# Transposing three more tiles by DMA in a fused chunked-attention and gated feed-forward kernel

## Chip, cores, metric

The kernel runs on one core of one Trainium2 chip, in one launch. The metric is device time in microseconds (us), the median of several runs. TensorE is called PE, VectorE DVE, ScalarE ACT, GpSimd POOL and SyncE SP, as in the profile. POOL, SP and ACT also issue the transfers (DMAs).

## What is computed

Attention over chunks of 32 positions, each with 16 positions to its left, 8 to its right and 8 memory positions, and then a feed-forward layer with a ReLU gate, on every position. 4 batches, 8 heads, 768 positions, head dimension 64; the feed-forward layer has width 512 and inner width 1536.

```python
for c in range(S // 32):
    q_c = q[:, :, 32*c:32*c+32]
    k_full = concat([mem_k, k[:, :, max(0, 32*c-16):min(S, 32*c+40)]], axis=2)
    v_full = concat([mem_v, v[:, :, max(0, 32*c-16):min(S, 32*c+40)]], axis=2)
    scores = q_c @ k_full.T / sqrt(D)
    scores = scores - max(scores)
    a = exp(scores); a = a / (sum(a) + 1e-9)
    out[:, :, 32*c:32*c+32] = a @ v_full
x = out.transpose(0, 2, 1, 3).reshape(B * S, H * D)
result = (relu(x @ w_gate) * (x @ w_val)) @ w_out
```

## The kernel before

The 3072 positions are 24 tiles of 128, six to a batch: tiles 0 to 5 are batch 0, 6 to 11 batch 1, 12 to 17 batch 2, 18 to 23 batch 3. For the feed-forward layer the tiles form eight blocks of 2, 2, 2, 4, 4, 4, 4 and 2 tiles; block 3 is tiles 6 to 9, block 4 tiles 10 to 13, block 5 tiles 14 to 17, block 6 tiles 18 to 21, block 7 tiles 22 and 23.

**Attention of a tile.** q and k are loaded by POOL with a cast to bf16 (`load_qk`, L250). Both must be transposed, so that the head dimension lies across the partitions. There are two ways. In the first, PE transposes by a product with the identity (`qk_t`, L271, four products for q and four for k) into PSUM, and ACT or DVE copies the result out (`qk_copy`, L285). In the second, a transposing DMA that SP issues (`qk_transfer`, L277) does it from on-chip memory to on-chip memory: q straight into `qT`, k into a staging tile `k_t` (three buffers), from which ACT or DVE copies it into the layout of `kT`. Tiles from `LATE_QK` on take the second way. The scores are 32 small products (`scores`, L297); the scores of tile a need k of tile a + 1 too, unless a is the last of its batch. Then come the row maximum, subtraction, exponential, sum, reciprocal and normalisation on DVE and ACT (L314 to L352). The result P is transposed in the same two ways: by PE and a copy (`p_t`, `p_copy`), or, from tile `LATE_P` on, by a transposing DMA (`p_transfer`, L360). `values` (L368) multiplies it by v, and `x_copy` puts the result into the block's xT.

**v.** For batches 1 to 3, v lies in one of two large buffers `v_bd`, used in turn. POOL loads it in four DMAs (`load_v_rows`, L182); then eight small DMAs (`mem_rows`, L164) put the memory rows in; then ACT or DVE copies 24 rows of each chunk up from the next one (`upper`, L190, sixteen copies a batch).

**Feed-forward of a block.** For each of 12 slices of the inner width, PE makes four products for the gate and four for the value (`first`, L401); ACT takes the ReLU (`relu`, L410) and DVE multiplies (`gate`, L415). At the end `second` (L427) makes the output products of every tile, in four groups of three, and ACT copies out and stores (`store`, L435). These products share four PSUM buffers.

**Order.** The order on every engine is fixed before the launch by a list scheduler inside the kernel (`schedule`, L682). It steps through a made-up time with a guessed duration of every operation and, on each engine, takes the ready operation of the best priority. PE, DVE, ACT and SP then run their lists strictly in that order, held by semaphores for true dependences only; the guessed times leave no trace but the order. POOL's order is the list `loads`, written out by hand (L639 to L675): the pairs and weights, then q and k of tile 6 to k of tile 8, the output weights, v of batch 1, then q and k up to k of tile 16, then v and memory rows of batch 2, then q and k of tiles 16 to 22, v and memory rows of batch 3, and the last three loads of q and k.

The names that the change touches:

- `LATE_QK`, `LATE_P` (L56): the tiles from which q, k and P are transposed by DMA.
- `pace` (L508): an operation after which a PE transpose of q or k may be placed: one that stands `LEAD` = 31 us of the planner's time ahead of the block's start.
- `pace_t` (L517): the same for a transposing DMA of tile a: not before the scores of tile a - 6 have been placed.
- `ISSUE`, `LAND`, `LAND_P` (L515): the planner's guesses of how long SP is busy with one transposing DMA, and how long after that its data is there. L770 is the guess of how much each one delays the loads.
- L674: which loads of q and k stand behind which batch's v in POOL's list.

Of the kernel before, what the change touches and what calls it, by code (L numbers as in the profile page):

```python
# [19 lines left out]
def kernel(  # L20
# [32 lines left out]
    BAND0 = 48  # L53
    UT = 3

    LATE_QK, LATE_P = 15, 15  # L56

    KEY_RUNS = ((0, CH, 0), (KW, 64, CH), (CH, KW, CTX))
    assert sum(BLOCKS) == NT and NMEM == 8 and D == 64 and H == 8
# [130 lines left out]
    def upper(b, par, i0, i1, eng):  # L190

        x = v_bd[b % NSET].rearrange("p h c d -> p (h c) d")
        d = slice(D * par, D * par + D)
        copy(eng, x[64 * par + CH:64 * par + CTX, i0:i1, d], x[64 * par:64 * par + CTX - CH, i0 + 1:i1 + 1, d])
# [232 lines left out]
    def second(blk, t, c, m0):  # L427
        st = FFN[blk]
        if m0 == 0:
            st["o", t, c] = fps.tile([128, c[1] - c[0]], F32, tag="fps", name="out_ps")  # L430
        for m in range(m0, m0 + MS):
            nc.tensor.matmul(st["o", t, c], lhsT=st["gv"][:, m, 128 * t:128 * t + 128],  # L432
                             rhs=w_out_sb[:, m, c[0]:c[1]], start=(m == 0), stop=(m == NDC - 1))

    def store(blk, t, c, eng):  # L435
        o = opool.tile([128, c[1] - c[0]], F32, name="o_sb")
        copy(eng, o, FFN[blk].pop(("o", t, c)))
        row = 128 * (starts[blk] + t)
        nc.scalar.dma_start(out[row:row + 128, c[0]:c[1]], o)


    starts = [sum(BLOCKS[:i]) for i in range(len(BLOCKS))]
# [8 lines left out]
    def op(key, eng, fn, deps=(), prio=(0,), take=(), give=(), after=()):  # L451
        ops[key] = dict(eng=eng, fn=fn, deps=list(deps), prio=prio, take=list(take), give=list(give),
                        after=list(after))

    def load(key, n, work, fn, deps=(), take=(), after=()):
        loads.append(dict(key=key, n=n, work=work, fn=fn, deps=list(deps), take=list(take), after=list(after)))
# [39 lines left out]
    LEAD, STEP, AHEAD = 31.0, 5.2, 10.0  # L496
    marks, clock, begun = [], 0.0, {}
# [9 lines left out]

    def pace(a):  # L508
        blk = block_of[a]
        at = begun[blk] - LEAD + STEP * (a - starts[blk]) - (AHEAD if a >= LATE_P else 0.0)  # L510
        gone = [key for c, key in marks if c <= at]
        return gone[-1:] if blk >= 2 else []


    ISSUE, LAND, SLACK, LAND_P = 1.4, 4.5, 1.0, 3.0  # L515

    def pace_t(a):  # L517
        return [("s", a - 6)]

    for a in range(NT):  # L520
        b, t = divmod(a, TPB)
# [48 lines left out]
        blk = block_of[a]  # L570
# [11 lines left out]
    for rank, (blk, m) in enumerate(seq):  # L582
# [11 lines left out]
        else:  # L594
            last = None
            for t, c in [(t, c) for t in range(n) for c in pieces(blk, t)]:
                for m0 in range(0, NDC, MS):
                    end = (t, c, m0) == (n - 1, pieces(blk, t)[-1], NDC - MS)
                    op(("o", blk, t, c, m0), {"PE": MS * 0.000422 * (c[1] - c[0])},
                       lambda e, blk=blk, t=t, c=c, m0=m0: second(blk, t, c, m0),  # L600
# [5 lines left out]
                   lambda e, blk=blk, t=t, c=c: store(blk, t, c, engine[e]), [last], (0.5, rank), ["o"],  # L606
# [11 lines left out]
    for b in range(1, B):  # L618
        for n in range(2 * HP):
            hp, par = divmod(n, 2)  # L620
            for m in range(TPB // UT):
# [3 lines left out]
                   lambda e, b=b, par=par, i0=i0, i1=i1: upper(b, par, i0, i1, engine[e]),  # L625
# [13 lines left out]
    late = [(a, i) for a in range(TPB, NT) for i in (1, 0)]  # L639
# [22 lines left out]
    for b in range(1, B):  # L662
        deps = ([("z0", hp, c0) for hp in range(HP) for c0 in range(0, NCH, 8)] if b > 1 else [("z1", hp) for hp in range(HP)]) + ([("v", TPB * (b - NSET + 1) - 1)] if b > NSET else [])
        if b == 1:
            for n in range(2 * HP):
                op(("mr", b, n), {"SP": 0.72}, lambda e, n=n: mem_rows(nc.sync, 1, n),
                   deps + [(("vm", 0), 0.2), (("vm", 1), 0.2)], (0,))
        for par in range(2):
            load_v_op(b, par, deps)
        if b > 1:  # L670
            for n in range(2 * HP):
                load(("mr", b, n), 192, 0.22, lambda b=b, n=n: mem_rows(nc.gpsimd, b, n),
                     deps + [(("vm", 0), 0.2), (("vm", 1), 0.2)])
        for a, i in late[5 if b == 1 else 9 + 12 * (b - 1):21 + 12 * (b - 1)]:  # L674
            load_qk_op(a, i)  # L675

    WARM = 18.0
# [4 lines left out]
    def schedule():  # L682
        done, started, times = {}, set(), [0.7]
        free = {e: 0.7 for e in ("PE", "ACT", "DVE", "SP", "POOL")}
        queue_end, flying, gives = 0.0, [], [(WARM + 0.15, "fps")]
# [28 lines left out]
        while len(started) < len(ops) + len(loads):  # L714
            t = heapq.heappop(times)
            while times and times[0] <= t + 1e-9:
                heapq.heappop(times)
            for g in [g for g in gives if g[0] <= t + 1e-9]:
                gives.remove(g)
                room[g[1]] += 1  # L720
            flying = [f for f in flying if f > t]
            moved = True
            while moved:
                moved = False
                for e in ("POOL", "PE", "ACT", "DVE", "SP"):
                    if free[e] > t + 1e-9:
                        continue
                    if e == "POOL":
                        if n_load == len(loads):
                            continue  # L730
                        o = loads[n_load]
                        if len(flying) >= 8 or not ready(o, t):
                            continue
                        n_load += 1
                        key = o["key"]
                        if o["n"]:
                            end = t + 0.62 + 0.27e-3 * o["n"]
                            queue_end = max(queue_end, end + 0.8) + o["work"]
                            flying.append(queue_end + 1.0)
                            done[key] = queue_end + (1.2 if n_load < 8 else 4.5 if key[:2] == ("vl", 1) else 2.4 if n_load < 45 else 6.0 if key[0] == "vl" else 4.0)  # L740
                        else:
                            end = done[key] = t + max(o["work"], 0.6)
                        fn = o["fn"]
                    else:
                        o = None
                        soon = False
                        for _, key in todo[e]:
                            late_pe = e == "PE" and t > 36.0 and ops[key]["prio"][0] == 1
                            if ready(ops[key], t, MARGIN if late_pe else 0.0):
                                o = None if soon and key[0] in ("up", "z0") else ops[key]  # L750
                                break
                            soon = soon or ready(ops[key], t + 0.3)
                        if o is None:
                            if e == "PE" and 1.3 < t < WARM:
                                order.append((t, lambda: idle_product(256)))
                                free[e] = t + (0.213 if t < 9.0 else 0.11)
                                heapq.heappush(times, free[e])
                            elif e == "PE" and t <= 1.3:
                                heapq.heappush(times, 1.31)
                            continue  # L760
                        for x in o["eng"]:
                            todo[x].remove((o["prio"], key))
                        d = o["eng"][e]
                        d, lat = d if isinstance(d, tuple) else (d, d)
                        d *= (1.8 if e == "PE" and t < 8.0 and key[0] in ("t", "p", "sh", "f") else 1.0)
                        end = t + d
                        done[key] = end + 0.25 if e == "PE" else t + lat + 0.08

                        if queue_end > t:
                            queue_end += 1.1 if e == "SP" and key[0] in ("t", "pc") else 0.7 if key[0] == "oc" else 0.0  # L770
                        fn = lambda o=o, e=e: o["fn"](e)
                        for g in o["give"]:
                            g, lag = g if isinstance(g, tuple) else (g, 0.0)
                            gives.append((done[key] + lag, g))
                            heapq.heappush(times, done[key] + lag)
                    for r in o["take"]:
                        room[r] -= 1
                    started.add(key)
                    for k in users.get(key, ()):
                        missing[k] -= 1  # L780
                        if not missing[k]:
                            offer(k)
                    order.append((t, fn))
                    free[e] = end
                    for x in (end, done[key], done[key] + 0.2, done[key] + 1.5, done[key] + MARGIN):
                        heapq.heappush(times, x)
                    moved = True
            assert times, [k for k in ops if k not in started][:20]
# [34 lines left out]
```

## Time and profile before

| | |
|---|---|
| median of 3 runs | 244.66 us (244.35 to 244.89) |
| the profiled execution | 244.74 us |
| its span, first to last instruction | 242.7 us |
| last product on PE ends | 239.6 us into the span |
| granted clock of PE, mean | 0.998 |
| PE busy | 235.8 us (97%) |
| DVE, ACT busy | 147.9 us, 136.0 us |
| POOL busy (it issues the loads) | 77.9 us |
| transposing DMAs on SP: q and k of tiles 15 to 23, P of the same | 18 and 9 |
| first and last of them issued | 71.98 us, 164.3 us |
| last load of q issued by POOL | 122.45 us |

The profile is one execution. "Idle before" gives what an engine waited for; a timeline lists instructions by start time, with the number merged into a line behind an x. A queue such as SPq or POOL lists the issue of a DMA, not its landing. A block's first products start at about 85.7 (block 3), 122.4 (block 4), 160.0 (block 5), 192.6 (block 6) and 223.7 us (block 7).

### The profile page before, as it was taken

What the parts mean: (1) busy time and instruction counts of PE and PEld (TensorE: products, weight loads), DVE (VectorE), ACT (ScalarE), POOL (GpSimd) and SP (SyncE); (2) the same over time, 40 slices, a digit from 0 to 9 for tenths busy, and PEclk for the clock granted to TensorE, in tenths of its full rate; (3) what the DMA queues carried; (4) which work ended last, traced back from release to release, by engine and by line L of the source; (5) the groups of instructions that cost most, each with busy time, mean ns of one, the idle gap of its engine ahead of it and who ended that gap; (6) DMA issues with size and microseconds to landing.
All of it is one profiled execution on the core that took longest, in us unless ns stands there. A gap on an engine that the chain in (4) does not pass through costs nothing.

```text
span 242.7 us, 6546 instructions
## 1 busy us (share of the span) xinstructions
PE 235.8 (97%) x2706; PEld 140.8 (58%) x2706; DVE 147.9 (61%) x296; ACT 136.0 (56%) x288; POOL 77.9 (32%) x102
## 2 busy tenths in 40 slices
PE   7898999999999999999999999999999999999994
PEld 5587887884589545554544545554445444445873
DVE  6674876988877458977549999894431043410430
ACT  7477777767885499665756674453332233312432
POOL 8975689235984396037430000000000000000000
PEclk9999999999999999999999999999999999999999
DMA  6999999999999999999990142651001210012102
GB/s 72 172 179 203 201 164 172 193 131 134 191 195 154 80 168 136 120 124 153 116 218 7 36 53 48 131 133 24 0 0 46 86 43 0 3 43 86 43 3 86
DMA packets 96413, 25.17 MB, mean 104 GB/s; under 512 B 87424, under 2 KB 93312, under 8 KB 96384
## 3 DMA queue, kind: packets, MB, share of 16 engines
q0 software_dynamic: 76128, 14.65, 83.5%
q1 hardware_dynamic: 16656, 3.82, 15.0%
q10 hardware_dynamic: 3600, 6.29, 8.1%
q8 instruction: 21, 0.34, 0.7%
q14 instruction: 8, 0.07, 0.1%
HBM read 28.55 MB, written 6.29 MB: 144 GB/s over the span
## 4 chain that ended last, share of the span: by engine, by line
PE 88%; ACT 4%; DMA 2%; POOL 2%; DVE 2%; issue 1%; ACTq 0%; POOLq 0%
PE v_ps L407 26%; PE g_ps L407 25%; PE out_ps L432 22%; PE xT_ps L388 3%; DMA v_n<-in_v_dram 2%; PE s_ps L309 2%; PE idle_ps L141 2%; PE vs_ps L215 2%; PE xT_ps L381 2%; PE pT_ps L358 2%; ACT v_bd L79 1%; PE qk_ps L275 1%; PE qk_ps L236 1%; POOL qk_p L227 1%; ACT o_sb L79 1%
## 5 line engine op out<-in xcount | busy, mean ns | idle before, releaser
L419 DVE TENSOR_TENSOR gvT<-v_ps,g_relu 128x256 f16<-128x256 f32 (+1 forms) x96 | 52.9, 554 | 58.2 <-PE v_ps L407 43.2
L407 PE MATMUL v_ps<-xT,w_val_sb 128*128 128x256 f16 (+1 forms) x384 | 78.2, 326 | 0.1
L407 PE MATMUL g_ps<-xT,w_gate_sb 128*128 128x256 f16 (+1 forms) x384 | 78.2, 326 | 0.0
L413 ACT ACTIVATE g_relu<-g_ps 128x256 f16<-128x256 f32 (+1 forms) x96 | 47.0, 491 | 47.6 <-PE g_ps L407 45.9
L432 PE MATMUL out_ps<-w_out_sb,gvT 128*128 128x512 f16 (+2 forms) x300 | 65.3, 371 | 0.0
L407 PEld LDWEIGHTS <-w_gate_sb 128*128 128x128 f16 x384 | 36.3, 98 | 23.1
L407 PEld LDWEIGHTS <-w_val_sb 128*128 128x128 f16 x384 | 36.0, 98 | 22.3 <-issue 0.5
L432 PEld LDWEIGHTS <-gvT 128*128 128x128 f16 x300 | 27.9, 98 | 29.9
L79 ACT COPY o_sb<-out_ps 128x512 f32<-128x512 f32 (+2 forms) x25 | 14.2, 567 | 31.8 <-PE out_ps L432 25.6
L337 ACT ACTIVATE p_exp<-dif 128x256 f16<-128x256 f32 (+2 forms) x72 | 19.6, 340 | 4.4 <-DVE dif L329 3.5
L322 DVE TENSOR_REDUCE mx<-s_ps 128x8 f32<-128x512 f32 x24 | 16.5, 688 | 5.6 <-PE s_ps L309 5.4
L341 DVE TENSOR_REDUCE sm<-p_exp 128x8 f32<-128x512 f16 x24 | 16.4, 683 | 4.4 <-ACT p_exp L337 4.1
L254 POOL DMA_DIRECT2D qk_b<-in_q_dram x18 | 16.4, 912 | 7.4 <-DMA v_bd<-in_v_dram 5.5
L254 POOL DMA_DIRECT2D qk_b<-in_k_dram x18 | 16.2, 903 | 5.5 <-DMA w_out_sb<-in_moe_w_out_dram 4.4
L79 ACT COPY v_bd<-v_bd 24x768 f16<-24x768 f16 (+1 forms) x20 | 15.6, 818 | 2.2 <-ACT o_sb L79 1.2
L352 DVE TENSOR_TENSOR p_n<-p_exp,rinv 128x512 f16<-128x512 f16 x24 | 16.5, 687 | 0.4
L329 DVE TENSOR_TENSOR dif<-s_ps,mx 128x512 f32<-128x512 f32 x24 | 16.4, 682 | 0.2
L185 POOL DMA_DIRECT2D v_bd<-in_v_dram x12 | 10.9, 920 | 12.5 <-PE v_ps L407 11.8
L168 POOL DMA_DIRECT2D v_bd<-vmem x16 | 10.5, 661 | 12.5 <-DMA v_bd<-in_v_dram 10.5
L79 ACT CAST xT<-xT_ps 128x512 f16<-128x512 f32 x17 | 9.9, 583 | 6.2 <-PE xT_ps L388 4.8
L141 PE MATMUL idle_ps<-idle 128*128 128x256 bf16 x69 | 11.5, 319 | 1.1 <-DVE warm L475 1.1
L388 PEld LDWEIGHTS <-v_bd 128*128 128x128 f16 x288 | 9.7, 96 | 3.2 <-issue 0.2
(57 smaller groups left out, 179.5 us busy)
## 6 DMA issues: line engine op xcount, KB each, us to landing
out_dram<-o_sb ACTq DMA_DIRECT2D x23, 256.0 KB
qk_b<-in_k_dram POOLq DMA_DIRECT2D x18, 128.0 KB, 7.2
qk_b<-in_q_dram POOLq DMA_DIRECT2D x18, 128.0 KB, 7.0
v_bd<-in_v_dram POOLq DMA_DIRECT2D x6, 384.0 KB, 11.5
w_out_sb<-in_moe_w_out_dram POOLq DMA_DIRECT2D x2, 768.0 KB, 10.5
qk_p<-in_k_dram POOLq DMA_DIRECT2D x3, 256.0 KB, 5.7
qk_p<-in_q_dram POOLq DMA_DIRECT2D x3, 256.0 KB, 6.6
v_n<-in_v_dram POOLq DMA_DIRECT2D x6, 128.0 KB, 6.5
```

The source lines that it names most:

```text
L79: nc.scalar.copy(o, i)
L254: nc.gpsimd.dma_start(qk_b[a, i], bass.AP(tensor=x.tensor, offset=x[b, 0, 128 * t, 0].offset, ap=[[D, 128], [S * D, H], [1, D]]))
L322: nc.vector.reduce_max(SM[a, "mx"], s4, axis=AX.X)
L329: nc.vector.tensor_tensor(out=SM[a, "dif"].rearrange("p (m r) a s -> p r m a s", r=2), in0=S_ps.pop(a).rearrange("p r (m a) s -> p r m a s ...
L337: nc.scalar.activation(p[:, :, :, s0:s0 + k1 - k0], dif[:, :, :, k0:k1], ACT.Exp, scale=SCALE)
L341: nc.vector.reduce_sum(SM[a, "sm"], SM[a, "p"], axis=AX.X)
L352: nc.vector.tensor_tensor(out=P_n[a], in0=SM.pop((a, "p")), in1=rinv_b, op=ALU.mult)
L388: nc.tensor.matmul(ps[:, hp, r], lhsT=v_bd[b % NSET][:, hp, 4 * t + g, :], rhs=x[:, hp, r], start=True, stop=True)
L407: nc.tensor.matmul(ps, lhsT=w[:, f, 128 * m:128 * m + 128], rhs=xTs[blk][:, f, :], start=(f == 0), stop=(f == NFC - 1))
L413: nc.scalar.activation(st["r", m], st.pop((0, m)), ACT.Relu)
L419: nc.vector.tensor_tensor(out=st["gv"][:, m, :], in0=st.pop((1, m)), in1=st.pop(("r", m)), op=ALU.mult)
L432: nc.tensor.matmul(st["o", t, c], lhsT=st["gv"][:, m, 128 * t:128 * t + 128], rhs=w_out_sb[:, m, c[0]:c[1]], start=(m == 0), stop=(m == ND ...
```

## The change

Tiles 12, 13 and 14, too, have q, k and P transposed by DMA: six more transposing DMAs of q and k and three of P, 36 in place of 27, and 36 products fewer on PE. In POOL's list, v and the memory rows of batch 2 move ahead of the nine loads from k of tile 12 to k of tile 16; all loads from tile 12 on to k of tile 22 now follow them in one run of 21. The PE transposes of tiles 10 and 11 may be placed 44 instead of 31 us of planner's time ahead of block 4, and a transposing DMA of tile a as soon as the scores of tile a - 3 are placed. Three guesses of the planner grow. It alone decides what follows for the order of all else.

```diff
-    LATE_QK, LATE_P = 15, 15
+    LATE_QK, LATE_P = 12, 12
...
     def pace(a):
         blk = block_of[a]
-        at = begun[blk] - LEAD + STEP * (a - starts[blk]) - (AHEAD if a >= LATE_P else 0.0)
+        at = begun[blk] - (44 if blk >= 4 else LEAD) + STEP * (a - starts[blk]) - (AHEAD if a >= LATE_P else 0.0)
         gone = [key for c, key in marks if c <= at]
         return gone[-1:] if blk >= 2 else []
...
-    ISSUE, LAND, SLACK, LAND_P = 1.4, 4.5, 1.0, 3.0
+    ISSUE, LAND, SLACK, LAND_P = 1.5, 6.0, 1.0, 6.0
...
     def pace_t(a):
-        return [("s", a - 6)]
+        return [("s", a - 3)]
...
-        for a, i in late[5 if b == 1 else 9 + 12 * (b - 1):21 + 12 * (b - 1)]:
+        for a, i in late[(5, 12, 33)[b - 1]:(12, 33, 36)[b - 1]]:
             load_qk_op(a, i)
...
                         if queue_end > t:
-                            queue_end += 1.1 if e == "SP" and key[0] in ("t", "pc") else 0.7 if key[0] == "oc" else 0.0
+                            queue_end += 1.5 if e == "SP" and key[0] in ("t", "pc") else 0.7 if key[0] == "oc" else 0.0
```

The order that results on PE, from block 3's last product on (f b,m: gate, value = the two product groups of slice m of block b; s, v, p: scores, values and PE transposes of P; t: PE transposes of q or k; o: output products):

```
before: o 3 (with p13, v13) | f 4,0 gate, t14q, value | f 4,1 | s14 | f 4,2 | f 4,3 gate, s15, value | ...
after:  o 3 (with v13, s16, s17, v14, v15) | f 4,0 gate, s18, value | f 4,1 | f 4,2 gate, v16, value, s19 | f 4,3 gate, v17, value | ...
```

And SP's list of transposing DMAs (k, q, P of a tile):

```
before: k15 q15 k16 q16 k17 q17 k18 q18 k19 q19 k20 q20 k21 q21 k22 q22 P15 k23 q23 P16 P17 ... P23
after:  k12 q12 k13 q13 k14 q14 k15 q15 k16 q16 P12 k17 P13 q17 k18 q18 P14 P15 k19 q19 k20 P16 q20 P17 k21 ...
```

## The prediction

> **What bounds the kernel now.** I read the page first (busy times, slices), then the chain of waits, then the timelines of POOL and SP, and last the DMA view of single stretches, for the transfers that the change adds to.
>
> ```profile
> span 242.7 us, 6546 instructions
> PE 235.8 (97%) x2706; PEld 140.8 (58%) x2706; DVE 147.9 (61%) x296; ACT 136.0 (56%) x288; POOL 77.9 (32%) x102
> DMA  6999999999999999999990142651001210012102
> ```
>
> PE has hardly any idle time; the other engines have much. DMA (40 slices of 6.07 us) is full to about 127 us and nearly empty after. The change takes work from the first and gives it to the second while that is full. The chain of waits from 120 to 135 us is PE alone:
>
> ```profile
> 122.57 0.86 PE g_ps L407 x4
> 123.43 0.22 PE qk_ps L275 x4
> 123.65 0.86 PE v_ps L407 x4
> ...
> 126.24 0.24 PE s_ps L309 x32
> 126.48 0.97 PE g_ps L407 x4
> ...
> 134.19 0.23 PE pT_ps L358 x4
> ```
>
> Four transposing products hold PE for 0.22 or 0.23 us, and nothing waits on either side. So work taken from PE here shortens the end by as much, as long as what PE needs next is there.
>
> **Part 1: 36 products off PE.** Six groups of q and k at 0.22 and three of P at 0.23: **2.0 us**. [...] The copies that go with them (ACT row of pT 586 ns, x3, and of qT) come off ACT and DVE, which are not the bound: nothing.
>
> **Part 2: tiles 10 and 11 sooner.** Their PE transposes and scores move from block 3's time (86.5 us on) into block 2's (about 72 to 81 us). PE is full in both, so the move itself is worth nothing. Their softmax (row maximum, subtraction, sum, normalisation at 0.69 each, the reciprocal at 0.2: 2.9 us of DVE a tile) goes along; DVE is busy 4.5 of the 8 us from 76 to 84, which hides it. Without that cover it would cost up to 5.8 - 3.5 = 2.3 us. I take 0.
>
> **Part 3: v of batch 2 past nine loads of q and k in POOL's queue.**
>
> ```profile
> 58.73 0.91 POOL L254 DMA_DIRECT2D qk_b<-in_k_dram  x1
> ...
> 67.46 3.80 POOL L185 DMA_DIRECT2D v_bd<-in_v_dram  x4 [0.52 <-DVE p_n L352]
> 71.25 0.67 POOL L168 DMA_DIRECT2D v_bd<-vmem  x1
> ...
> 84.26 0.92 POOL L254 DMA_DIRECT2D qk_b<-in_q_dram  x1
> ```
>
> The first line is k of tile 12, the last q of tile 16. The zeroing that v waits for ends on DVE at 55.6, so v can be issued at 58.7, four DMAs in 3.8 us. Then come the memory rows, which wait for v to land, as they do here (four waits, 10.5 us). Loads alone bring 11801 packets in the 12 us from 56 to 68, 983 a us; v is 6144 packets, so 6.3 us after q of tile 11 (landed 64.4 by the completion records), plus a latency of 1.3: about 72. So k of tile 12 is issued near 72.7 (71 to 75) and lands 4.3 later, at 77, as q of tile 16 does here (84.26, landed 88.6). It then stands where q of tile 16 stands now, 11.5 us sooner. Nothing on PE is due from it before 90: 0.
>
> **Part 4: the transposing DMAs, at the time when the loads run.** SP's timeline and the DMA view of the stretches 92 to 100 (loads and transposes) and 102 to 110 us (loads running out), in this order:
>
> ```profile
> 88.63 1.22 SPq L283 DMA_TRANSPOSE qT<-qk_b  x1
> 89.94 1.29 SPq L283 DMA_TRANSPOSE k_t<-qk_b  x1
> 91.32 1.80 SPq L283 DMA_TRANSPOSE qT<-qk_b  x1
> ...
> q0 software_dynamic: 5242, 0.66, 142.5%
> q1 hardware_dynamic: 1857, 0.45, 54.3%
> ...
> q1 hardware_dynamic: 3233, 0.79, 97.8%
> q0 software_dynamic: 2401, 0.30, 58.6%
> ```
>
> SP can issue one in 1.2 us. What the DMA engines do is slower: q1 is SP's queue, and a transpose is 544 packets (3264 for the six that ran between 137 and 152 us). From 92 to 100 that is 1857/544 = 3.4 in 8 us, **2.34 us each**; from 102 to 110, with fewer loads, 5.9, 1.35 us each. Over 92 to 104, a pause of a us included, it is 2620 packets, 2.49 us each; beside v of batch 2 (76.5 to 83.7) 1622, 2.41 us each. The first of a row lands 6 us after issue (q of tile 16: 88.63, landed 94.5).
>
> In the kernel before that was slow enough for no one: q and k of tile 15 were issued at 72 for scores at 129. In the changed order there is a due time. By SP's list the 22nd transposing DMA is P of tile 16, the 24th P of tile 17. When does PE get there? Block 4 begins at 122.40 now. By then PE has lost seven groups (1.6 us) and gained four scores at 0.24 + 0.11 = 0.35 and two values at 0.40 (2.2 us): 123.0. Five product groups at 0.86 and one scores lead to values of tile 16: 127.7. Another values, scores and two groups to those of tile 17: 130.2.
>
> The first transposing DMA, k of tile 12, lands at about 83. So the 22nd is in time if each takes (127.7 - 83)/21 = 2.13 us, the 24th at (130.2 - 83)/23 = 2.05. The loads do not thin out before: after 83 there are some 16 of q and k (1024 packets each), v of batch 3 (6144), its memory rows and three more loads, 27,000 packets at 5242/8 = 655 a us beside transposes, or 588 over 92 to 104: to 124 or 129 us. With 2.34 us each to 129 (20.7 landed) and 1.35 after, the 22nd lands at 130.8 and the 24th at 133.5: late by 3.1 and 3.3. The lateness is not added up, since whatever stalls PE gives all later ones that time. So PE **stands 3.3 us** before values of tile 17, in one place or in several. I take 2.34, because that stretch has both queues busy throughout and no pause. Bounds: at 2.05 or less nothing, as in the row of 1.35; at 2.49, with loads to 130, the 22nd lands at 132.9 and the 24th at 135.6: 5.4.
>
> Behind the late transposes stand: on ACT and DVE, in order, the copies from `k_t` and all ReLUs and gates behind them; on PE everything. SP's queue also holds P of a tile ahead of the next tiles' q and k, but these are issued well before they can be served, so that costs nothing.
>
> **Sum.** -2.0 + 3.3 = +1.3 us. The profiled execution took 244.74 (span 242.7 and 2.0 around it), 0.08 above the median; I add to the median 244.66: **246.0 us**.
>
> **Rivals.**
> - *The transposes keep up* (2.05 us or less each): 244.66 - 2.0 = 242.7. For it: the ten landings from q of tile 16 (94.5) to q of tile 20 (109.8) are 1.7 us apart on average, and a lone one takes 0.8 us of packets. Against: the second half of these ran after the loads had thinned out, and the change puts 21 loads, not 12, beside them. [...]
> - *The stall equals the gain.* v of batch 3 follows the 21 loads at once. 16 of them from 83 at 588 a us end at 110.9, its two halves 5.2 each later plus 1.3: 117.4 and 122.6. The 16 copies of L190 stand on DVE and ACT behind P of tile 16's normalisation, from about 118.5 and 124.5 on; a freeze of the queues like that in 100 to 102 makes them 1 to 2 us late, and DVE holds the gates up meanwhile. With transposes in time, or nearly so: -2.0 + 2.0 = 244.7.
> - *The pauses count in full*, 2.49 us each: 244.66 - 2.0 + 5.4 = 248.1. It is the upper end of the forecast's own case.
> - *PE stands earlier, at scores of tile 12*, if v of batch 2 comes late: q of tile 12, the second, lands at 85.5 and is due near 92.7 (two blocks of work ahead of it as now). 7 us of room; I give it no share of its own.
>
> **Chances.** Forecast 0.56 (246.0, its own range 245.2 to 248.4, with the pauses in it), transposes keep up 0.33, stall and gain equal 0.11. Runs spread by 0.1%, so 0.2%, 0.5 us, is what can be told from no change. Faster 0.34, same 0.10, slower 0.56. The rate decides, and each 0.1 us of it is worth 2.3 us at the 24th; so the range reaches from the full gain to the row with the pauses, with 0.2 to 0.3 us for the scatter of runs: 242.5 to 248.4.
>
> **What will show it.** PE products of L275 x48 and L358 x48 (72 and 60 now), SP transposes 36. Right, if PE has idle time ahead of values (xT_ps) or scores between 112 and 140 us, released by the transposing DMA or by a copy of `k_t`, some 3 us in all, and q1 has near 1857 packets per 8 us while q0 runs. Wrong, if PE is unbroken from 70 us on (the gain of 2.0 stands), or if the waits fall on `upper` copies, or if v of batch 2 makes scores of tile 12 late.

## The result, and the profile after

The changed kernel takes 252.42 us (median of 6, 250.21 to 255.70) where the one before takes 244.63: the ratio is 1.028, with a 95% interval of 1.024 to 1.033. Forecast were 246.0 us. The ratios, other than the medians, leave out every execution more than 1.5% above the fastest of its kernel: here two of six, the profiled one (254.93 us) among them, in e10 three of twelve and in e7 three of ten. So the trace is read for where the time goes, and sizes are taken from ratios: 2.8% of 244.6 is **6.9 us** (7.8 by the medians).

The page of the changed kernel (busy times; 40 slices of 6.3 us; granted clock):

```profile
span 253.0 us, 6475 instructions
PE 237.7 (94%) x2670; PEld 139.4 (55%) x2670; DVE 145.6 (58%) x289; ACT 137.8 (54%) x289; POOL 77.3 (31%) x102
PE   7998999999999999899677799999999999999994
PEclk9999999999999999999959999999999999999999
```

PE is no longer unbroken. 36 products are gone (2670 for 2706), but the slices from 120 to 145 us are at 6 and 7 tenths, and in one of them the granted clock is at half. The windows of 124 to 128 and 128 to 135 us (length, then busy time and count of PE, PEld, DVE, ACT, POOL, then clock, DMA share, GB/s):

```profile
124.00:128.00 4.00, 0.42 (x10) 0.24 (x10) 0.59 (x3) 0.59 (x1) 0.00 (x0) 0.78 1.26 135
128.00:135.00 7.00, 5.27 (x58) 1.94 (x55) 0.65 (x2) 1.12 (x3) 3.97 (x5) 0.64 1.49 111
```

PE's timeline there (start, duration, instruction, and in brackets the idle time before it with its releaser):

```profile
121.44 2.75 PE L432 MATMUL out_ps<-w_out_sb,gvT 128*128 128x512 f16 x12
127.76 0.61 PE L388 MATMUL xT_ps<-pT,v_bd 128*128 128x32 f16 x16 [3.58 <-DMA pT<-p_n]
128.21 2.72 PE L432 MATMUL out_ps<-w_out_sb,gvT 128*128 128x512 f16 x6
130.72 1.91 PE L407 MATMUL g_ps<-xT,w_gate_sb 128*128 128x512 f16 x4
132.56 0.25 PE L309 MATMUL s_ps<-kT,qT 64*32 64x48 bf16 x6
134.54 0.29 PE L309 MATMUL s_ps<-kT,qT 64*32 64x64 bf16 x26 [1.73 <-ACT kT L79]
134.77 1.04 PE L407 MATMUL v_ps<-xT,w_val_sb 128*128 128x512 f16 x4
```

PE stands 3.58 us ahead of values of tile 15, whose P comes by DMA, and then 1.73 us ahead of scores. Between the two, six output products take 2.72 us, where twelve took 2.75 just before, and a gate group 1.91, where the value group at 134.77, four products of the same shape, takes 1.04. Further waits, all ahead of scores, are 0.99 us at 103.6, 0.41 at 108.2 and 1.33 at 141.1: 8.0 us with the two shown. All lie between block 3's first product (87.7 us, 85.7 before) and block 5's (170.0, 160.0 before); from there to the end both kernels need the same time (79.5 and 79.6 us).

Two timelines say more. ACT's, at the same time:

```profile
124.01 0.59 ACT L79 COPY o_sb<-out_ps 128x512 f32<-128x512 f32 x1
133.46 0.37 ACTq L439 DMA_DIRECT2D out_dram<-o_sb  x1
133.87 0.62 ACT L79 COPY kT<-k_t 128x512 bf16<-128x512 bf16 x1 [9.27 <-DMA qT<-qk_b]
```

ACT copied block 3's third output tile at 124.0 and could issue its store only at 133.46. What it waited for is put down to a transfer into `qT`, which neither the store nor the copy behind it reads. And SP's, where the L283 lines are transfers of k (into `k_t`) and q (into `qT`):

```profile
86.00 1.48 SPq L283 DMA_TRANSPOSE qT<-qk_b  x1
94.07 1.19 SPq L283 DMA_TRANSPOSE k_t<-qk_b  x1
97.72 1.19 SPq L283 DMA_TRANSPOSE qT<-qk_b  x1
```

SP issued nothing for 6.6 us after q of tile 14. The trace's records explain both holes. They name, for every DMA, the semaphore whose updates come as it lands, and for every instruction the semaphores that it waits for. The 73 DMAs of SP and ACT have one of eight such completion semaphores each, and none of the 73 was issued while an earlier one with the same semaphore was under way: in all 65 cases of a semaphore used again, the issuing engine has, between the two issues, an instruction that waits for it. Four were issued right when the earlier one landed:

```
DMA held                issued   semaphore  held by                    landed
SP   k of tile 15        94.07   108        ACT store, block 2, first    93.93
SP   q of tile 15        97.72   111        ACT store, block 2, second   97.66
SP   k of tile 21       132.92   115        SP  k of tile 19            132.81
ACT  store, block 3, 3rd 133.46  116        SP  q of tile 19            133.39
```

Not all of both holes is the semaphores' alone. SP could not have issued k of tile 15 before 89.08, when DVE had emptied its `k_t` buffer, so 5.0 of the 6.6 us are theirs; the hold of k of tile 21 cost 0.1, since SP was busy to 132.75. And the copy behind ACT's store needs k of tile 19, which landed only at 132.81, so the store's semaphore kept ACT only 0.6 us longer than that copy would have.

In the kernel before, SP and ACT share eight semaphores too, and none of their 64 DMAs was held by one. But POOL has eight of its own, and there 31 of 96 DMAs were issued within 0.3 us of a landing on their semaphore. The sign stood in POOL's timeline before the change:

```profile
72.24 1.39 POOL L168 DMA_DIRECT2D v_bd<-vmem  x2 [0.33 <-DMA qk_b<-in_k_dram]
77.11 1.25 POOL L168 DMA_DIRECT2D v_bd<-vmem  x2 [1.68 <-DMA v_bd<-in_v_dram]
```

These memory rows don't read `qk_b`, and they don't wait for v either: the first four were issued from 71.25 to 74.80, and v's first DMA landed at 76.83. So the description of the order given above is wrong in one point: the lists are not held for true dependences only. The planner allows POOL eight loads under way (`len(flying) >= 8`, L732); for SP and ACT it has no such limit.

So there were two theories for the lost time besides the forecast's (transposing DMAs too slow beside loads): the shared semaphores, and due times that the planner set too early. It planned 7.5 us from the start of an issue to the landing (1.5 and 6.0), and for the 27 transposing DMAs issued up to 136 us 5.9 to 14.9 us passed, over 7.6 for 19 of them.

### The profile page after: what moved, and what is told of

It is laid out like the page before. It is cut to its first block, busy times and chain, and to the rows that moved or that the text cites. A ratio compares the mean times of both kernels' runs of the same rounds, so it can differ in the third digit from the quotient of the medians.

```text
span 253.0 us, 6475 instructions
## 1 busy us (share of the span) xinstructions
PE 237.7 (94%) x2670; PEld 139.4 (55%) x2670; DVE 145.6 (58%) x289; ACT 137.8 (54%) x289; POOL 77.3 (31%) x102
## 4 chain that ended last, share of the span: by engine, by line
PE 69%; DMA 14%; ACT 8%; issue 3%; DVE 2%; POOL 1%; ACTq 1%; SPq 1%; POOLq 0%
PE v_ps L407 20%; PE g_ps L407 20%; PE out_ps L432 17%; DMA k_t<-qk_b 7%; DMA qT<-qk_b 6%; ACT v_bd L79 3%; DMA v_n<-in_v_dram 2%; PE idle_ps L141 2%; PE s_ps L309 2%; PE vs_ps L215 2%; PE xT_ps L388 2%; PE xT_ps L381 1%; ACT g_relu L413 1%; ACT o_sb L79 1%; PE pT_ps L358 1%
## 5 line engine op out<-in xcount | busy, mean ns | idle before, releaser
L407 PE MATMUL g_ps<-xT,w_gate_sb 128*128 128x256 f16 (+1 forms) x384 | 79.1, 329 | 0.0
L432 PE MATMUL out_ps<-w_out_sb,gvT 128*128 128x512 f16 (+2 forms) x300 | 67.1, 375 | 0.0
L79 ACT COPY v_bd<-v_bd 24x768 f16<-24x768 f16 (+1 forms) x23 | 18.5, 816 | 1.6 <-ACT o_sb L79 1.2
L79 ACT CAST xT<-xT_ps 128x512 f16<-128x512 f32 x18 | 10.5, 585 | 7.8 <-PE xT_ps L388 6.6
L388 PE MATMUL xT_ps<-pT,v_bd 128*128 128x32 f16 x288 | 10.0, 177 | 3.7 <-DMA pT<-p_n 3.6
L79 ACT COPY kT<-k_t 128x512 bf16<-128x512 bf16 x9 | 5.5, 613 | 14.5 <-DMA qT<-qk_b 9.3
```

What stands on the lines that cost most here:

```text
L79: nc.scalar.copy(o, i)
L388: nc.tensor.matmul(ps[:, hp, r], lhsT=v_bd[b % NSET][:, hp, 4 * t + g, :], rhs=x[:, hp, r], start=True, stop=True)
L407: nc.tensor.matmul(ps, lhsT=w[:, f, 128 * m:128 * m + 128], rhs=xTs[blk][:, f, :], start=(f == 0), stop=(f == NFC - 1))
```

## The experiments

All runs stand against the kernel before on the same chip (244.4 to 244.8 us).

| run | edit to the changed kernel | median, us | ratio, 95% interval | over before, us |
|---|---|---|---|---|
| | the change itself | 252.42 | 1.0282 (1.0239 to 1.0325) | +6.9 |
| e1 | no transfer moved | 245.88 | 1.0070 (1.0046 to 1.0095) | +1.7 |
| e2 | stores of block 2 later | 251.02 | 1.0260 (1.0228 to 1.0292) | +6.4 |
| e3 | 9 and 10 us planned | 246.08 | 1.0081 (1.0041 to 1.0122) | +2.0 |
| e4 | e2 and e3 | 247.26 | 1.0106 (1.0068 to 1.0144) | +2.6 |
| e5 | no memory rows of batch 3 | 251.28 | 1.0285 (1.0265 to 1.0305) | +7.0 |
| e6 | no v of batch 3 | 248.15 | 1.0154 (1.0119 to 1.0189) | +3.8 |
| e7 | e3, memory rows behind three loads | 245.74 | 1.0029 (1.0000 to 1.0058) | +0.7 |
| e8 | e2, 10 us planned, memory rows behind three loads | 248.28 | 1.0151 (1.0133 to 1.0169) | +3.7 |
| e9 | stores of blocks 2, 3 on POOL's queue | 248.89 | 1.0177 (1.0135 to 1.0219) | +4.3 |
| e10 | e9 and e3 | 244.58 | 0.9980 (0.9958 to 1.0002) | -0.5 |
| e11 | e9, 10 us planned | 243.48 | 0.9950 (0.9936 to 0.9964) | -1.2 |
| e12 | P of tiles 12 to 14 back on PE | 248.38 | 1.0139 (1.0105 to 1.0173) | +3.4 |
| e13 | kernel before, lead of 44 alone | 249.62 | 1.0204 (1.0166 to 1.0242) | +5.0 |
| e14 | kernel before, loads' order alone | 245.15 | 1.0019 (0.9999 to 1.0040) | +0.5 |

The last column is the ratio less one, times 244.5.

### e1: the change without its moved transfers

```diff
-    LATE_QK, LATE_P = 12, 12
+    LATE_QK, LATE_P = 15, 15
```

> The change without its moved transposes: LATE_QK and LATE_P stay 15, so k, q and P of tiles 12 to 14 are transposed on TensorE as before; the order of the loads, the lead of 44 and the planner's constants are those of the change. If the nine moved groups of tile 12 to 14 alone cost the time, this comes out where the kernel before does, 244.6 us (244.2 to 245.5), with no idle time of PE over 0.5 us between 90 and 150 us. Rival: the loads' order or the sooner tiles 10 and 11 cost it (v of batch 2 past nine loads, v of batch 3 behind 21); then 248 us or more.

245.88 us. After 23 us no wait of PE is longer than 0.25, so the rest, 5.2 of 6.9 us, comes with the moved transfers. But 1.7 us are lost without them; the median is above the range expected. PE is busy 19.4 of the 20 us from 68 to 88 us, where it was 19.75 before; that is 0.3 of it.

### e2: the stores of block 2 later

```diff
+    STORE_LAG = 10.0
...
-        nc.scalar.dma_start(out[row:row + 128, c[0]:c[1]], o)
+        if blk != 2:
+            nc.scalar.dma_start(out[row:row + 128, c[0]:c[1]], o)
+        else:
+            TMP["o", t] = row, o
...
+                if blk == 2:
+                    op(("od", t), {"ACT": 0.06}, lambda e, t=t: store_late(t), [(("oc", blk, t, c), STORE_LAG)], (0.5, rank), (),
+                       [("o", 2.5)])
```

The DMA becomes an operation of its own on ACT, placed 10 us of planner's time after the copy.

> The change, with the two stores of block 2 issued from their own place in ACT's list, 10 us later than their copies (nothing else moves). In the changed kernel the transfer of k of tile 15 was issued 8.1 us after the one ahead of it, and its completion semaphore is the one that block 2's first store raised when it landed at 93.9 us. Theory of the shared semaphore: that transfer is issued near 89 us, five us sooner, PE's waits of 1.0 and 0.4 us ahead of scores at 103 and 108 us go, the 3.6 us ahead of values at 128 us falls to 1 or less with the stretch of half clock behind it: 246 to 248.5 us. Theory of the rate (transposing DMAs too slow beside loads, memory rows and stores, whenever they are issued): at most 1.5 us better than the change, 250.5 us or more.

The mechanism held and the size did not. k of tile 15 was issued at 88.30 instead of 94.07, and PE's waits at 103 and 108 us were gone. But values of tile 15 still waited 3.25 us at 125.4, and the time is 251.02 us, where the theory had 248.5 at most: 0.5 better by the ratios, whose intervals overlap. Block 2's stores by themselves are a small part at most. Block 3's third store was still held, for q of tile 19 (landed 130.13, store issued 130.21), 3.4 us longer than for k of tile 19 (landed 126.75), which the copy behind it needs.

### e3: a longer time planned for each transposing DMA

```diff
-    ISSUE, LAND, SLACK, LAND_P = 1.5, 6.0, 1.0, 6.0
+    ISSUE, LAND, SLACK, LAND_P = 1.5, 9.0, 1.0, 10.0
```

> The change with the planner's guess of a transposing DMA's time raised from 6.0 to 9.0 us (q, k) and 10.0 us (P); nothing is taken away, the planner only puts what uses them later in each engine's list. Theory of the early due times: 5.4 to 13.4 us passed from issue to landing where 6.0 was planned, and in-order engines stood; with 9 and 10 the waits of PE fall from 8 us to 1 to 3 us and no half clock follows: 244 to 247.5 us. Rival (the transfers come late in any order, and PE stands elsewhere): 249 us or more.

246.08 us: as expected, 4.9 us come back from the order alone, with every transfer still there. The plan is not longer for it (its last store stays at 237.5 us of planner's time), so values of tile 15 had no need to stand at 121 in it. In the plan of e3 they stand 8 us later, at 129, with block 4's products, work that the kernel has anyway, ahead of them; block 5, which uses them, begins at 157. One wait was left; ACT and PE in this run:

```profile
119.01 0.58 ACT L79 COPY o_sb<-out_ps 128x512 f32<-128x512 f32 x1 [0.33 <-PE out_ps L432]
125.35 0.34 ACTq L439 DMA_DIRECT2D out_dram<-o_sb  x1
125.73 1.63 ACT L79 COPY v_bd<-v_bd 24x704 f16<-24x704 f16 x2 [6.13 <-DMA out_dram<-o_sb]
...
128.02 1.02 PE L407 MATMUL v_ps<-xT,w_val_sb 128*128 128x512 f16 x4 [2.78 <-ACT o_sb L79]
```

ACT stands in block 3's third store again, this time for the first store (semaphore 112, landed 125.28). PE stands 2.78 us behind it, for the PSUM buffer that ACT's next copy of an output tile frees. (That copy needs the first store's landing in any case, for there are three `o_sb` buffers.)

### e4: both

> Both edits: the stores of block 2 later, and 9.0 and 10.0 us planned for a transposing DMA. If the shared semaphore and the early due times make up the loss, PE runs unbroken and the 2.0 us of the 36 products off PE are left: 242.7 to 244.5 us. If the rate of the transposing DMAs between 121 and 131 us (2.4 to 3.3 us each) is a bound of its own, P of tile 15 and q of tile 19 come late again, and it takes 246 us or more.

247.26 us, no better than e3. The number and the transfers are those of the theory of the rate (P of tile 15 landed at 127.5, q of tile 19 at 133.0), but in the profiled execution PE is unbroken but for 0.42 us, since what uses them stands later now. That execution was the lowest of four, and what the slower ones waited for is not recorded. The run settles nothing.

### e5: no memory rows of batch 3

```diff
-                load(("mr", b, n), 192, 0.22, lambda b=b, n=n: mem_rows(nc.gpsimd, b, n),
+                load(("mr", b, n), 192, 0.22, lambda b=b, n=n: mem_rows(nc.gpsimd, b, n) if b < 3 else None,
```

> The change without the eight DMAs of batch 3's memory rows (v_bd<-vmem, on-chip, 8 partitions each; tiles 18 to 23 then attend with batch 1's memory values). In the changed kernel these run from 123 us on, few packets of 3072 bytes, and the transposing DMAs beside them take 2.4 to 3.3 us each, against 1.4 to 1.9 beside loads. Theory of the memory rows: without them P of tile 15, issued near 115, lands by 122 to 123, the wait of 3.6 us ahead of values at 128 us goes below 1, no half clock follows it: 246 to 248.5 us. Rival, the packets of the loads (v, q, k of batch 3): the wait stays at 3 us or more, 250.5 us or more.

251.28 us: the theory of the memory rows falls as a cause of the time, though its prediction of the transfer nearly came true. P of tile 15 landed at 123.3 instead of 127.7:

```profile
123.36 0.57 PE L388 MATMUL xT_ps<-pT,v_bd 128*128 128x32 f16 x16 [1.00 <-DMA pT<-p_n]
...
129.14 0.40 PE L309 MATMUL s_ps<-kT,qT 64*32 64x64 bf16 x26 [2.90 <-ACT kT L79]
```

PE's first wait shrinks to 1.00 us and a new one of 2.90 takes its place 6 us later: ACT stood 4.6 us in block 3's third store, for q of tile 19 (semaphore 116; landed 127.97, store issued 128.04). One limit lifted, the next one holds. Here the store's semaphore does cost what it seems to: k of tile 19, which the copy behind the store needs, had landed at 124.10.

### e6: no loads of v of batch 3

```diff
-        load(("vl", b, par), CH * n, CH * n * 1.03e-3, lambda: load_v_rows(b, par, 0, CH, 0, n), (), (), deps)
+        load(("vl", b, par), CH * n, CH * n * 1.03e-3, lambda: load_v_rows(b, par, 0, CH, 0, n) if b < 3 else None, (), (), deps)
...
```

> The change without the loads of v of batch 3 (6144 packets of 128 bytes and two small DMAs; tiles 18 to 23 then use batch 1's v), its memory rows kept. Theory of the load packets, as in the prediction (2.34 us for a transposing DMA beside loads): with a quarter of the packets after 83 us gone the transposes keep up and PE's waits after 110 us fall to 1 us or less: 245 to 247.5 us. Theory of the memory rows: these now stand right behind q and k in the queue and run 5 to 8 us sooner; the slow stretch (2.4 us or more for one transposing DMA) moves with them to 108 to 120 us and PE stands there instead: 249 us or more.

248.15 us, between the two. Fewer packets help: 3.1 us. The memory rows, now sooner, also do what their theory said: P of tiles 12 and 13 landed at 111.3 and 115.7 us (issued 101.8, 104.8), and PE stood 1.66 and 0.73 us for them. Both slow the transfers; neither is the whole.

### e7 and e8: memory rows later in POOL's list

```diff
+        if b == 3:
+            for a, i in late[33:]:
+                load_qk_op(a, i)
...
-                     deps + [(("vm", 0), 0.2), (("vm", 1), 0.2)])
+                     deps + [(("vm", 0), 0.2), (("vm", 1), 0.2)] + ([("pc", 17)] if b == 3 else []))
...
```

e7 has this with the planned times of e3, e8 with 10 us for all and block 2's stores as in e2.

> 9.0 and 10.0 us planned for a transposing DMA, as in the third run, and the eight DMAs of batch 3's memory rows put behind the transfer of P of tile 17 and behind the last three loads in POOL's queue (issued near 136 us; values of tile 18 need them at 150). Theory of the memory rows: no stretch of 2.4 us or more for one transposing DMA before 136 us, block 4's first product group at 122 and block 5's at 157.5 to 159 us: 243.5 to 245 us. Rival (they matter little, the loads alone do it): no better than the third run, 245.5 us or more.

> Stores of block 2 later, 10.0 us planned for every transposing DMA, memory rows of batch 3 behind P of tile 17. If due times and memory rows together are the loss, PE runs unbroken from 23 us on and the 2.0 us of the 36 products are left: 242.7 to 244.2 us, below the kernel before. If some 1.4 us of loss belongs to the order of the loads (the first run, 245.9 us with no transfer moved), it stays there too: 244.3 to 246 us.

The edit did less than it said. The dependence on P of tile 17 is one of the planner's alone; it orders POOL's list and makes POOL wait for nothing, so the rows were issued from 110.7 us in e7 and 107.8 in e8, only behind three more loads. 245.74 us in e7 is not clear of e3, whose interval overlaps its own, and the theory was not tested. e8 came out at 248.28, above all that was expected, and shows why. ACT:

```profile
119.79 0.59 ACT L79 COPY o_sb<-out_ps 128x512 f32<-128x512 f32 x1
123.62 0.34 ACTq L441 DMA_DIRECT2D out_dram<-o_sb  x1
124.00 0.83 ACT L79 COPY v_bd<-v_bd 24x768 f16<-24x768 f16 x1 [3.63 <-DMA k_t<-qk_b]
```

Block 3's third store stood 3.2 us for k of tile 18 (semaphore 108, landed 123.55). Behind it ACT had the copy of xT, and PE stood 3.19 us for that at 125.5, ahead of block 4's first product. Tile 15's values waited for nothing here. The wait behind the store is the only one of PE over 0.35 us in the trace after 23 us, and the half clock that followed it (0.61 on average from 126 to 129 us) comes on top; the time is 3.7 over.

### e9: the stores of blocks 2 and 3 off the shared semaphores

```diff
-        o = opool.tile([128, c[1] - c[0]], F32, name="o_sb")
+        n = starts[blk] + t - 4
+        if blk in (2, 3):
+            o = qk_p[n % 2, n // 2].rearrange("p h d -> p (h d)").bitcast(F32)
+        else:
+            o = opool.tile([128, c[1] - c[0]], F32, name="o_sb")
...
-        nc.scalar.dma_start(out[row:row + 128, c[0]:c[1]], o)
+        (nc.gpsimd if blk in (2, 3) else nc.scalar).dma_start(out[row:row + 128, c[0]:c[1]], o)
```

> The change, with the six stores of blocks 2 and 3 issued from POOL's queue instead of ACT's, out of buffers that are free by then (qk_p of batch 0); every engine's order stays. In the changed kernel ACT stood from 124.6 to 133.5 us in block 3's third store: it was issued when the transfer of q of tile 19 landed (133.4), whose completion semaphore it shares, and SP's transfer of k of tile 15 stood for block 2's first store in the same way. Theory of the shared semaphores: with no store among them ACT never stands behind a transfer that it has no use for; PE's waits ahead of scores (1.0, 0.4, 1.7, 1.3 us) go, those ahead of values of tile 15 (3.6 us, and the half clock after it) stay as long as its due time is early: 247.5 to 249.5 us. Rival (the transfers' rate sets everything, the semaphores only show it): 251 us or more.

248.89 us, as expected. No DMA of SP or ACT was issued right after another's landing on its semaphore any more. All waits ahead of scores are gone, and one wait of PE is left:

```profile
124.79 0.56 PE L388 MATMUL xT_ps<-pT,v_bd 128*128 128x32 f16 x16 [2.84 <-DMA pT<-p_n]
125.20 1.68 PE L432 MATMUL out_ps<-w_out_sb,gvT 128*128 128x512 f16 x6
126.67 1.91 PE L407 MATMUL g_ps<-xT,w_gate_sb 128*128 128x512 f16 x4
```

That is values of tile 15 at their early place, with slow products behind them. The edit does two more things: it takes six issues of some 0.35 us off ACT and gives these stores buffers of their own, where three were shared. So the 2.6 us between the change and e9 belong to all three. The buffers held nothing in the change (the fourth copy came at 135.79, and the first store had landed at 127.0), and ACT is not the bound; that nearly all of the 2.6 is the semaphores' is argued from this.

### e10 and e11: both causes taken away

e10 is e9 with 9.0 and 10.0 us planned, e11 with 10.0 for all.

```diff
-    ISSUE, LAND, SLACK, LAND_P = 1.5, 6.0, 1.0, 6.0
+    ISSUE, LAND, SLACK, LAND_P = 1.5, 10.0, 1.0, 10.0
```

> The stores of blocks 2 and 3 from POOL's queue, and 9.0 and 10.0 us planned for a transposing DMA. In the third run (the planned times alone, 246.1 us) one wait of PE was left, 2.8 us ahead of a product group at 128 us behind a copy of ACT, which stood 6.1 us for a store. Theory of due times and shared semaphores together: that wait goes, PE runs unbroken from 23 us on: 242.8 to 244.2 us, below the kernel before. If the transfers' rate still bounds, or the loads' order costs its 1.4 us of the first run: 244.8 us or more.

> The same with 10.0 us planned for every transposing DMA (k, q and P). The plan is as long as with 9.0, so by the theory of due times and shared semaphores it gives the same time within 0.5 us, 242.8 to 244.2; the seventh and eighth runs differed by 2.5 us at these values only because ACT stood 3.2 us in a store. Rival (10.0 itself was what hurt in the eighth run): 246 us or more.

e11 takes 243.48 us (243.02 to 244.48), as expected, 0.5% less than the kernel before (interval 0.36 to 0.64%): with both edits the change beats the kernel before by 1.2 us. Whether the stores on POOL would also make the kernel before faster was not run. Its page:

```profile
span 242.7 us, 6468 instructions
PE 233.7 (96%) x2670; PEld 137.8 (57%) x2670; DVE 144.7 (60%) x286; ACT 139.1 (57%) x292; POOL 81.1 (33%) x108
PE   7897999999999999999989999999999999999994
PEclk9999999999999999999999999999999999999999
```

PE is nearly unbroken (waits of 0.81 and 0.45 us are left), and the clock is whole. e10 has a median of 244.58, above the 244.2 expected; it reaches 243.14 at best, but its runs go up to 250.4 and its interval touches no change. That it stands closer to the edge, with a us less planned for q and k, is a guess: only its fastest execution has a trace. By the ratios the stores' edit gives 2.5 us on e3 (e10), as on the change.

### e12: P of tiles 12 to 14 back on PE

```diff
-    LATE_QK, LATE_P = 12, 12
+    LATE_QK, LATE_P = 12, 15
```

> The change with LATE_P back at 15: P of tiles 12 to 14 is transposed on TensorE again, q and k of these tiles by DMA. Three transposing DMAs fewer between 102 and 121 us, 0.7 us more of PE. If the transfers' rate decides (22 of them in time or not), the ones due at 123 to 128 us come some 4 to 5 us sooner and the time falls to 246.5 to 248.5 us. If the stores' semaphores and the early due times decide, it stays at 250 us or more.

248.38 us, in the range that the rate has. P of tile 15 landed at 123.6 and its values, due 123.7 here, waited for nothing. Two waits of 1.0 and 1.1 us ahead of scores remain, behind ACT's copy from `k_t` and DVE's subtraction. Four DMAs were held by semaphores here too, and the plan is another, so the run doesn't part the rate from the due times.

### e13 and e14: the lead and the loads' order by themselves

```diff
-        at = begun[blk] - LEAD + STEP * (a - starts[blk]) - (AHEAD if a >= LATE_P else 0.0)
+        at = begun[blk] - (44 if blk >= 4 else LEAD) + STEP * (a - starts[blk]) - (AHEAD if a >= LATE_P else 0.0)
```

(e13, on the kernel before; e14 has the loads' order of the diff instead.)

> The kernel before with the lead of 44 for blocks 4 on and nothing else: tiles 10 and 11 are begun in block 2's time. Theory: the 1.4 us of the first run come from here, PE meets more short waits around scores and copies between 68 and 90 us, where it has tiles 10 and 11 beside its product groups (19.4 of 20 us busy in the first run, 19.75 before): 245.4 to 246.3 us. Rival (the loads' order costs it): 244.3 to 245.0 us.

> The kernel before with the changed order of loads alone: twelve loads of q and k ahead of v of batch 2 instead of 21, 21 ahead of v of batch 3. Theory of the lead: nothing on PE waits for these loads, 244.3 to 245.0 us. Rival (v of batch 3 and its copies come late and hold ACT and DVE): 245.4 us or more, with idle time of PE between 105 and 135 us.

The loads' order alone gives 245.15 us, between its two forecasts, and between no change and 0.4% slower. The lead alone costs 5.0 us, outside both forecasts (246.3 at most) and far more than in e1, where it has the loads' order and the longer planned times beside it. In e13, ACT:

```profile
85.11 0.62 ACT L79 COPY kT<-k_t 128x512 bf16<-128x512 bf16 x1 [3.07 <-DMA k_t<-qk_b]
```

k of tile 15 was issued at 73.42 and landed at 85.1, 11.7 us later where 5.9 were planned. ACT's exponential stood behind this copy, DVE's next sum and copy of q behind the exponential, and PE stood 1.90 us at 88.5. So a lead that looks like a rearrangement on PE moves a transfer's due time as well. The two parts can't be added up.

## Why the prediction was wrong

The direction was right and the size was not: +1.3 us forecast, +6.9 measured. The signs that it named came (PE standing ahead of values and scores between 112 and 140 us), but with 5.3 us where it had some 3. By its steps:

- **Part 1, 2.0 us off PE**: nothing speaks against it. The 36 products are gone, nine groups of four at 0.22 us each, and e11, with the waits nearly gone, lies 1.2 us below the kernel before. No run measures the 2.0 by itself.
- **Part 2 and Part 3, nothing**: v of batch 2 and k of tile 12 came where they were put (k issued at 74.5 and landed at 77.8; forecast 72.7 and 77). But nothing was the wrong price: together with the new planned times these parts cost 1.7 us (e1), and e13 shows that the lead alone can cost 5. Part 3 also took the memory rows to wait for v; their waits were for semaphores, as above.
- **Part 4, the rate**: right as a mean, in part by luck. 2.34 us for a transposing DMA were read from the row of 92 to 100 us. In e9, where no store holds SP, k of tile 12 landed at 80.7 and P of tile 17, 23 transfers later, at 133.5 (first landing records): 2.29 us each. P of tile 16 landed at 129.7, forecast 130.8; P of tile 17 at 133.5 as forecast. But the mean is not a steady rate: up to q of tile 16 (101.3) it is 2.29; then SP issues nothing from 95.2 to 99.75, until P of tile 12 is there; from 107.0 to 118.2 it is 1.6, with the loads still running, and after that 2.2 with one gap of 4.8. (The rival's row of landings holds nine, not ten, so 1.9 us apart and not 1.7.)
- **Part 4, which transfer is late**: the steps looked at the 22nd and 24th. The 18th, P of tile 15, was due sooner, at 121.9 us in e9 (124.79 less its 2.84 of waiting); by the same rate it lands at 83 + 17 x 2.34 = 122.8, 0.9 late. The wait of **2.84 us** in e9 has the size of the forecast 3.3, in another place, and that is luck: P of tile 15 came after the gap of 4.8 us and had all landed only at 124.74.
- **The step that failed** first of all is the one sentence on the queue, "these are issued well before they can be served, so that costs nothing", and with it the list of what stands behind the late transposes. It took a queue to be held by data alone, as the account of the kernel before did. Shared completion semaphores held SP's queue for ACT's stores and ACT's for SP's transfers: with the six stores on POOL's queue 6.9 fell to e9's 4.3, **2.6 us**, the largest term that the sum lacks. The nothing of Parts 2 and 3, 1.7 us, is the next.
- **Left out of the sum**: what a wait does to the products after it. In e9 the 2.84 us were followed by 1.68, 1.91 and 1.44 us for work that takes 1.46, 1.03 and 1.03 ahead of any wait in e3, **1.5 us**.

-2.0 + 2.84 + 1.5 + 1.7 = 4.0 for e9, which measured 4.3; with the semaphores' 2.6 that is 6.6 of 6.9. That it comes so near proves little, since the terms are from different kernels: e9's profiled execution took 247.67 us, only 2.9 more than the kernel before, and e11, which has the lead, the loads' order and longer planned times too, keeps 1.2 of the 2.0. The 1.7 is the least certain. The rivals: *transposes keep up* was wrong, by the rate. *The stall equals the gain* was wrong: v of batch 3 landed later than its step had it (120.0 and 128.4 us, forecast 117.4 and 122.6), but no wait of PE falls on `upper`. *The pauses count in full* came nearer in time for another reason. Scores of tile 12 waited for nothing.

What the forecast did not ask at all is whether the due time was real. It compared landings with PE's list as if that were fixed by need. e3 put the same operations later in the same list, values of tile 15 by 8 us of planner's time, and got 4.9 us back.

## What to carry to other kernels

When work goes from an engine to a queue, read two things beside the queue's rate: where the consumer stands in its engine's list and when its result is really needed. Here PE, which runs its list in order, stood for an early place as much as for a late transfer: later places alone gave 4.9 us back (e3). And look at what else shares a DMA's completion semaphore: here a store whose semaphore a slower transfer still had was issued only at 133.46 us, and ACT did nothing from 124.60 on for something that the store doesn't read. The profile then named a releaser that made no sense for the instruction (a transfer into `qT`, for a copy from `k_t`), which is the sign to look for. And set a planner's guess of a latency from what the loaded stretch shows: here 9 or 10 us after the issue served where 6.0 had been taken and most transfers took longer (19 of 27 over 7.6 us from the start of the issue, where 7.5 were planned); more than 10 was not tried.

## What the runs showed of the hardware

- **The granted clock fell around waits of 1.90 us and more.** In all eight traces where PE waited 1.90 us or more at once after 23 us (1.90 us in e13, 1.99 in e14, 2.78 in e3, 2.84 in e9, 2.90 in e5, 3.19 in e8, 3.25 in e2, 3.58 in the change) the clock records stand at half for 3.4 us, in e5 and the change for 6.8; they begin between 1.6 us before the wait's end (the change) and 1.5 after it (e9). With waits up to 1.73 us (the change, at 134.5) the clock stayed whole. The shortest of the eight, 1.90 us in e13, came after a stretch without a pause: PE was busy for all of the 2.61 us from 84.00 us to that wait.
- **The wait for a semaphore sat on the issuing engine.** In the change an instruction of ACT that waits for semaphore 116 stands at 133.41 us, right ahead of block 3's third store. The transfer of q of tile 19 updated that semaphore last at 133.39, the store was issued at 133.46, and ACT did nothing from 124.60 to 133.41 us.
- **What a transposing DMA of 128 KB took depended on what ran beside it.** Over 23 of them in e9 it was 2.3 us each. From 106 to 114 us of the change they landed 1.5 us apart, beside some 4300 load packets. Between 120.8 and 126.2 us none landed at all, with 261 load packets in the 8 us from 122 on. What ran then was the memory rows of batch 3 (packets of 3072 bytes to 8 partitions) and block 3's stores. Without the rows P of tile 15 landed 4.4 us sooner (e5: 123.3, the change: 127.7); the stores' part was not measured.
